# Later chunks of A in four column groups, seven combine-weight transposes ahead of the MLP loop, conversions ahead of half steps

## The chip, the cores and the metric

The kernel runs on one core of a Trainium2 chip. The metric is device time in microseconds, the median of several runs; lower is better.

## The reference, cut to what matters

Three layers follow one another, all in 32-bit floats.

```python
x = attention(q, k, v)               # 4 batches, 8 heads, 576 tokens, head size 64; masked, strided
x = x.reshape(2304, 512)             # N = 2304 tokens, D = 512
logits = x @ phi                     # 32 slots = 8 experts x 4
slot_input = softmax(logits, axis=0).T @ x
slot_out[e] = relu(slot_input[e] @ w1[e]) @ w2[e]       # 8 experts, F = 1024
c = softmax(logits, axis=1)          # combine weights, 2304 x 32
x = c @ slot_out                     # slot_out is 32 x 512
h = relu(x @ w_in)                   # d_ff = 2048
out = (h * h) @ w_out                # 2304 x 512
```

Since x is `c @ slot_out`, the kernel never forms it for the MLP. It forms A = slot_out @ w_in, which has 32 rows and 2048 columns, and takes h = relu(c @ A).

## The kernel before, in words

**Ahead of the loop.** Attention and the slot softmax come first, then the experts, two at a time, by `layer1` and `layer2` in the order of the list `order` (line 1140). The last call, `layer2(3)`, leaves slot_out in `so`, and from it four small matmuls (line 1076) and two ScalarE copies make `soT`, slot_out transposed, in which every slot stands twice (32 + 32 columns). Fillers, matmuls whose result nobody reads, stand where TensorE waits for copies: `fill(4)` (lines 1066 and 1081) and `fill(6)` (line 1127); in the profile they are line 165.

**A in chunks.** A is made in four chunks of 512 columns, numbered c. `a_chunk(c, tag)` (line 1113) multiplies `soT` (64 columns, both copies) with the chunk's w_in tiles `wi[c]` in two column groups (line 1120), and ScalarE and VectorE leave `A4[c]`: in its upper 64 rows A rounded to fp32r, twice, and in its lower 64 rows the remainder, twice (lines 1133 and 1135). Chunk 0 is made ahead of the loop in two parts, the chunk c+1 inside it, after step 8 of the twelve steps of chunk c (line 1247).

**Combine weights.** `c_parts(chf, b)` (line 1005, GpSimd, two copies) lays out the weights of batch b, rounded part and remainder side by side, in a tile `c4` of which there are two. `c_transpose(b, t0, t1)` (line 1011) transposes them on TensorE (line 1016) and one copy (line 1020) puts them into `cT4`. The list `CP` (line 1139) holds the eight calls, two for each batch. Three come ahead of the loop, the other five after the steps 0, 1, 4, 5 and 6 (`TR`, line 1173).

**The loop.** There are 48 steps n (line 1214): four chunks c, three blocks `sb` of 768 tokens, and in each block four tiles f of 128 rows of d_ff. One step is 18 matmuls of line 1229: six token tiles t, and for each the products rounded x rounded, rounded x remainder, remainder x rounded. What a step multiplies was made by `emit_h` (line 1180) in two halves of 384 tokens each: one matmul of A with cT (line 1190), then ScalarE for relu, square and rounding (lines 1197, 1203, 1205), then VectorE for the remainder (line 1206). Halves are made ahead: at t = 1 and t = 4 of step n those of step n+1 (second half) and n+2 (first half).

**Conversions.** The weights come as 64-bit floats. `conv_late` (line 1107) turns one tile into 32 bits: one GpSimd instruction into a scratch tile nm (line 220; two such tiles) and three of VectorE (lines 223, 224, 227); I call these four a conversion. For a tile of w_out `conv_split` (line 1100) later splits it on GpSimd into rounded part and remainder (lines 1104 and 1105), which the step that uses it first waits for. There is one conversion in each of eight of the twelve steps of a chunk (`CONV`, line 1174): the four tiles of w_in for the next chunk at the steps 2, 4, 5, 6, then w_out tiles at 8, 9, 10 and, for the fourth step of the next chunk, at its step 1. From step 2 on they are issued at t = 4, behind the half made there.

**Order.** From `layer2(3)` on, `pin` (line 100) makes every compute engine issue its instructions in the order in which the code names them, except those between a `pin()` and a `pin(free=True)`, which the scheduler may place: the first three transposes (line 1158) are such. So an instruction that waits holds up all behind it on its engine.

Of the kernel before, what the change touches and what calls it, by code (L numbers as in the profile page):

```python
# [7 lines left out]
F32 = mybir.dt.float32  # L8
F32R = mybir.dt.float32r
# [28 lines left out]
def kernel(  # L38
# [61 lines left out]
    def pin(free=False):  # L100
        traced = nc.cur_bb.bb.instructions
        for i in traced[mark[0]:]:
            if free or i.engine not in COMPUTE:
                continue
            prev = last_of.get(i.engine)
            if prev is not None:
                tc.add_manual_dep(
                    i, prev,
                    mybir.DependencyInfo(mybir.DependencyClass.NoSync, mybir.DependencyReason.DATA),
                    reason="issue order",  # L110
                )
            last_of[i.engine] = i.name
        mark[0] = len(traced)
# [14 lines left out]
    def psum(tag):  # L128
        n = nt[tag] = nt.get(tag, -1) + 1
        return banks[:, 2 * ("s", "o", "t1", "t2").index(tag) + n % 2]  # L130
# [31 lines left out]
    def fill(n, ins):  # L162
        ps = psum("s")
        for _ in range(n):
            new = nc.tensor.matmul(
                out=ps[:, 0:256], lhsT=identb, rhs=fillb, start=True, stop=True
            )
            behind(new, ins)
            ins = new
# [160 lines left out]
    wi = {}  # L330
# [674 lines left out]
    def c_parts(chf, b):  # L1005

        c4 = c4s[b] = tail.tile([128, 5, 2, 2, 32], F32, tag="c4", name="c4", bufs=2)
        for i, src in enumerate((chf, cl_)):
            nc.gpsimd.tensor_copy(c4[:, :, :, i], src[:, 5 * b:5 * b + 5, None, :].to_broadcast([128, 5, 2, 32]))

    def c_transpose(b, t0, t1):
        c4 = c4s[b]
        ps = psum("t2")
        n = min(t1 * 128, S) - t0 * 128
        for t in range(t0, t1):
            nc.tensor.transpose(
                out=ps[:, ts(t - t0, 128)], in_=c4[:, t].rearrange("p h a s -> p (h a s)"), identity=ident
            )
        c0 = b * S + t0 * 128
        (nc.vector.tensor_copy if b == 0 else nc.scalar.copy)(out=cT4[:, c0:c0 + n], in_=ps[:, 0:n])  # L1020


    hTs, acc2 = {}, []
# [24 lines left out]
    def layer2(pr):  # L1048
        hT = hTs.pop(pr)
        if pr == 0:  # L1050
            acc2.extend(psum("t1") for _ in range(2))
        if pr == NP - 1:
            so = tail.tile([128, 512], F32, tag="hs", name="so", bufs=2)
        for f2 in range(2):
            for i in range(2):
                for fc in (2 * f2, 2 * f2 + 1):
                    for g in range(4):
                        w = wt[("w2", 2 * pr + g // 2, 2 * (g % 2) + f2)]
                        c0 = 512 * (fc % 2) + 256 * i
                        ins = nc.tensor.matmul(  # L1060
                            out=acc2[i][ts(g, 32), 0:256], lhsT=hT[:, fc, ts(g, 32)], rhs=w[:, c0:c0 + 256],
                            start=(pr == 0 and fc == 0), stop=(pr == NP - 1 and fc == 3),
                            tile_position=(0, 32 * g),
                        )
                if (pr, f2, i) == (NP - 1, 1, 1):
                    fill(4, ins)
                if pr == NP - 1 and f2:
                    nc.scalar.copy(out=so[:, ts(i, 256)], in_=acc2[i][:, 0:256])
            done(*[("w2", 2 * pr + ee, 2 * fh + f2) for ee in range(2) for fh in range(2)])
            fetch()  # L1070
        if pr < NP - 1:
            return
        for i in range(2):
            ps = psum("o")
            for k in range(2):
                ins = nc.tensor.matmul(
                    out=ps[:, ts(k, 64)], lhsT=so[:, ts(2 * i + k, 128)],
                    rhs=same[:, 0:2].rearrange("p a s -> p (a s)"), start=True, stop=True,
                )
            if i:  # L1080
                fill(4, ins)
            nc.scalar.copy(out=soT[:, 2 * i:2 * i + 2].rearrange("p k a s -> p (k a s)"), in_=ps[:, 0:128])


    split = []
# [21 lines left out]
    def conv_late(early=False):  # L1107
        if todo or early:
            (conv_in if todo[0][0] == "in" else lambda: conv_out(early))()
            fetch()  # L1110


    def a_chunk(c, tag, n0=0, n1=2):
        two = tag == "o"
        pss = [psum(tag)[:, 0:(n1 - n0) * 128] for _ in range(1 + two)]
        both = [(n, ii) for n in range(n0, n1) for ii in (((0,), (1,)) if two else ((0, 1),))]
        for n, ii in both:
            for kt in range(KD):
                for i in ii:
                    ins = nc.tensor.matmul(  # L1120
                        out=pss[i * two][ts(i, 64), ts(n - n0, 128)],
                        lhsT=soT[:, kt].rearrange("p a s -> p (a s)"),
                        rhs=wi[c][kt][:, ts(2 * n + i, 128)],
                        start=(kt == 0), stop=(kt == KD - 1), tile_position=(0, 64 * i),
                    )
        if c == 0 and n0 == 0:
            fill(6, ins)
        if n0 == 0:
            A4[c] = mp.tile([128, 512], F32R, tag="A4", name="A4", bufs=2)
        cv = A4[c].rearrange("p (s i w) -> p i s w", i=2, w=128)[:, :, n0:n1]  # L1130
        pv = [p.rearrange("p (s w) -> p s w", w=128) for p in pss]
        for i in range(2):
            nc.scalar.copy(out=cv[0:64, i], in_=pv[i * two][ts(i, 64)])
        for i in range(2):
            nc.vector.tensor_tensor(
                out=cv[64:128, i], in0=pv[i * two][ts(i, 64)], in1=cv[0:64, i].bitcast(F32), op=ALU.subtract
            )

    CP = [(b, t0, t1) for b in range(B) for t0, t1 in ((0, 3), (3, 5))]
    for layer, pr in order:  # L1140
        if (layer, pr) == (2, NP - 1):

            pin(free=True)
            conv_late(True)
        (layer1, layer2)[layer - 1](pr)
        if (layer, pr) == (2, 0):
            chf = c_softmax()
            for b in range(2):
                c_parts(chf, b)
# [6 lines left out]
    cT4 = mp.tile([128, NT], F32R, name="cT4")  # L1156
    for x in CP[0:3]:
        c_transpose(*x)
    pin(free=True)
    part = mp.tile([128, NT // 128, 512], F32, name="part")  # L1160
    A4 = {}
    conv_split()
# [7 lines left out]
    seq = [(c, sb, QF * c + j) for c in range(NC) for sb in range(NSB) for j in range(QF)]  # L1170
    gs = {}

    TR = (0, 1, 4, 5, 6)
    CONV = [j for j in range(1, 3 * QF - 1) if j % QF != QF - 1]


# [30 lines left out]

    emit_h()
    conv_late()
    c_parts(chf, 2)  # L1210
    emit_h()
    a_chunk(0, "t1", 1, 2)
    acc = None
    for n, (c, sb, f) in enumerate(seq):
        gh, gl = gs.pop(n)
        first, last = f % QF == 0, f % QF == QF - 1
        j = n % (NSB * QF)
        if first:
            acc = [psum(a) for a in ("s", "s", "o", "o", "t1", "t1")]
        for t in range(TB):  # L1220
            if t == 1 or t == (5 if n == 0 else 4) or (n, t) == (0, 3):
                emit_h()
            if t == 1:
                conv_split()
            elif t == (2 if n < 2 else 4):
                if n < QF - 2 or j in CONV:
                    conv_late()
            for k, (a, w) in enumerate(((gh, 0), (gh, 1), (gl, 0))):
                nc.tensor.matmul(  # L1229
                    out=acc[t], lhsT=a[:, ts(t, 128)], rhs=wo[f][:, ts(w, 512)],  # L1230
                    start=(first and k == 0), stop=(last and k == 2),
                )
            if not last:
                continue

            r = sb * TB + t
            pt = part[:, r]
            nh = 2 if n == len(seq) - 1 and t == TB - 1 else 1
            for i in range(nh):
                cs = ts(i, 512 // nh)  # L1240
                if c == 0:
                    (nc.vector.tensor_copy if t % 2 else nc.scalar.copy)(out=pt, in_=acc[t])
                else:
                    nc.vector.tensor_tensor(out=pt[:, cs], in0=acc[t][:, cs], in1=pt[:, cs], op=ALU.add)  # L1244
                if c == NC - 1:
                    nc.sync.dma_start(out=out[128 * r:128 * r + 128, cs], in_=pt[:, cs])
        if j == 3 * QF - 4 and c < NC - 1:
            a_chunk(c + 1, "t2")
        if n == 3:
            c_parts(chf, 3)  # L1250
        if n in TR:
            c_transpose(*CP[3 + TR.index(n)])
    pin()


# [28 lines left out]
```

## Time and profile before

| | |
|---|---|
| median of 3 runs | 415.74 us (413.55 to 416.15) |
| the profiled execution | 418.53 us, of which 416.8 us from first to last instruction |
| busy: TensorE, VectorE, ScalarE, GpSimd | 387.3, 242.6, 226.7, 90.8 us |
| TensorE clock granted, mean | 0.979 of full speed |
| matmuls of line 1229 | 864, 218.3 us busy |
| DMA traffic | 69.88 MB |

PE is TensorE's matmuls, PEld its weight loads, DVE is VectorE, ACT ScalarE, POOL GpSimd, SP the queue that issues the DMAs. Matmuls overlap, so that their busy times can add up to more than the time that passed; the chain of waits gives the time that passed. The loop lasts from 186 to 410 us. In a stage that TensorE fills, work on another engine counts only where TensorE waits for it.

### The profile page before, as it was taken

The page shows a single profiled execution, that of the slowest core. Times are in us where ns is not written, and L with a number is a line of the kernel's source. Part 1 is how long each engine was busy: PE and PEld are TensorE (multiplying, and loading weights), DVE is VectorE, ACT ScalarE, POOL GpSimd, SP SyncE. Part 2 cuts the span into 40 slices and gives each one's busy share as a digit, 9 for nine tenths or more (in the row PEclk, how much of TensorE's full clock was granted, in tenths as well). Part 3 has the DMA queues.
Part 4 walks back from the last instruction along what each step waited for, and adds up shares of the span by engine and source line. Part 5 has one row for each costly group of instructions (what it writes and reads, how often), then busy time and mean ns, then how long its engine had stood idle before and what let it go on. Part 6 is the DMA issues. An engine that isn't in the chain of part 4 may idle for free.

```text
span 416.8 us, 9152 instructions
## 1 busy us (share of the span) xinstructions
PE 387.3 (93%) x3654; PEld 302.3 (73%) x3654; DVE 242.6 (58%) x453; ACT 226.7 (54%) x459; POOL 90.8 (22%) x128
## 2 busy tenths in 40 slices
PE   6887798889699899999999999999999999999996
PEld 3776576777587645467788887888887888878884
DVE  6565547765265561138866564867657776745434
ACT  3452627536345220039778686666666676666760
POOL 6302211112022020035600252111414103420000
PEclk9998979999799999999999999999999999999999
DMA  6898898998999999997212131221000000003033
GB/s 153 234 251 227 215 227 300 210 293 203 274 384 270 395 333 417 417 417 309 87 64 102 51 103 58 95 101 50 2 0 1 2 0 2 1 0 153 37 116 151
DMA packets 52203, 69.88 MB, mean 168 GB/s; under 512 B 31744, under 2 KB 37120, under 8 KB 52160
## 3 DMA queue, kind: packets, MB, share of 16 engines
q1 hardware_dynamic: 52160, 69.29, 52.2%
q8 instruction: 29, 0.48, 0.5%
q14 instruction: 14, 0.11, 0.1%
HBM read 64.55 MB, written 4.72 MB: 166 GB/s over the span
## 4 chain that ended last, share of the span: by engine, by line
PE 73%; DMA 9%; DVE 5%; POOL 4%; ACT 3%; SPq 3%; issue 2%; POOLq 0%; DVEq 0%; ACTq 0%
PE banks L1229 43%; DMA space<-in_v_dram 6%; PE banks L1060 4%; PE banks L1190 4%; PE banks L1030 3%; PE banks L501 2%; DMA w<-in_moe_w_dram 2%; PE banks L554 2%; PE banks L1120 2%; PE banks L665 1%; PE banks L673 1%; POOL w L1105 1%; PE banks L728 1%; PE banks L734 1%; POOL space L410 1%
## 5 line engine op out<-in xcount | busy, mean ns | idle before, releaser
L1229 PE MATMUL banks<-w 128*128 128x512 f32 x864 | 218.3, 394 | 1.6 <-POOL w L1105 1.2
L1229 PEld LDWEIGHTS banks<-w 128*128 128x128 f32 x864 | 159.3, 188 | 37.2 <-POOL w L1105 2.9
L1206 DVE TENSOR_TENSOR w<-r,w 128x384 fp32r<-128x384 f32 (+1 forms) x97 | 57.8, 598 | 72.4 <-ACT w L1205 72.3
L1197 ACT ACTIVATE r<-banks 128x384 f32<-128x384 f32 (+1 forms) x96 | 47.0, 490 | 53.0 <-PE banks L1190 43.6
L1203 ACT ACTIVATE r<-r 128x384 f32<-128x384 f32 (+1 forms) x96 | 50.3, 524 | 3.0
L1205 ACT CAST w<-r 128x384 fp32r<-128x384 f32 (+1 forms) x97 | 49.5, 510 | 4.1 <-DVE r L1202 0.5
L488 ACT COPY space<-banks 64x576 f32<-64x576 f32 (+2 forms) x64 | 34.8, 543 | 19.5 <-PE banks L153 12.2
L220 POOL TENSOR_SCALAR nm<-w 128x512 f32<-128x512 f32 x28 | 23.5, 843 | 63.0 <-DMA w<-in_moe_w_out_dram 31.9
L1244 DVE TENSOR_TENSOR part<-banks,part 128x512 f32<-128x512 f32 (+1 forms) x55 | 34.9, 673 | 2.4 <-PE banks L1229 2.3
L410 POOL COPY space<-space 32x1088 f32<-32x1088 f32 x16 | 17.5, 1096 | 80.9 <-DMA space<-in_v_dram 57.6
L1104 POOL CAST w<-wf 128x512 fp32r<-128x512 f32 x16 | 11.8, 740 | 94.8 <-PE banks L1229 37.2
L1190 PE MATMUL banks<-cT,A 128*128 128x384 f32 x96 | 32.0, 335 | 0.0
L501 PE MATMUL banks<-ident,space 128*128 128x128 f32 x128 | 21.9, 297 | 1.6 <-DMA space<-in_q_dram 1.6
L224 DVE SCALAR_TENSOR_TENSOR nm<-w,nm 128x512 uint32<-128x512 uint32 x32 | 22.3, 696 | 1.1
L223 DVE TENSOR_SCALAR nm<-nm 128x512 uint32<-128x512 uint32 x32 | 14.6, 457 | 12.5 <-POOL nm L220 8.7
L1105 POOL TENSOR_TENSOR w<-wf,w 128x512 fp32r<-128x512 f32 x16 | 21.4, 1339 | 1.4
L525 ACT ACTIVATE space<-banks 128x576 f32<-128x576 f32 x16 | 10.4, 651 | 20.1 <-PE banks L506 15.9
L1190 PEld LDWEIGHTS banks<-cT,A 128*128 128x128 f32 x96 | 18.0, 188 | 3.9 <-ACT r L1197 0.2
L488 DVE COPY space<-banks 128x576 f32<-128x576 f32 (+1 forms) x16 | 9.7, 608 | 17.3 <-ACT space L488 13.5
L501 PEld LDWEIGHTS banks<-ident,space 128*128 128x128 f32 x128 | 15.7, 159 | 4.7 <-POOL w L437 2.5
L665 PE MATMUL banks<-space 128*32 128x130 f32 x288 | 13.0, 294 | 5.6 <-POOL space L410 3.7
L665 PEld LDWEIGHTS banks<-space 128*32 128x32 f32 x288 | 9.5, 116 | 7.7 <-POOL space L410 4.7
(186 smaller groups left out, 450.4 us busy)
## 6 DMA issues: line engine op xcount, KB each, us to landing
w<-in_moe_w_dram SPq DMA_DIRECT2D x48, 512.0 KB, 7.3
w<-in_moe_w_in_dram SPq DMA_DIRECT2D x16, 512.0 KB
space<-in_moe_w_dram SPq DMA_DIRECT2D x16, 512.0 KB, 7.4
w<-in_moe_w_out_dram SPq DMA_DIRECT2D x16, 512.0 KB, 6.6
space<-in_v_dram SPq DMA_DIRECT2D x32, 144.0 KB, 7.5
out_dram<-part SPq DMA_DIRECT2D x17, 256.0 KB, 2.0
space<-in_k_dram SPq DMA_DIRECT2D x16, 128.0 KB, 2.9
space<-in_q_dram SPq DMA_DIRECT2D x16, 128.0 KB, 2.6
```

Source lines behind the costliest of these rows:

```text
L220: nc.gpsimd.tensor_scalar(out=m, in0=hf, scalar1=2.0 ** -112, scalar2=1.0, op0=ALU.mult, op1=ALU.mult)
L488: return (nc.scalar.copy if act else nc.vector.tensor_copy)(out=out, in_=in_)
L501: nc.tensor.transpose(out=pf[:, w * t:w * t + 128], in_=m[:, ts(t, 128)], identity=ident)
L665: nc.tensor.matmul(out=pv[c, n // 4] if n < 18 else pv[c, 4].rearrange("p (h e) -> p h e", h=2), lhsT=w, rhs=i, start=True, stop=True, til ...
L1105: nc.gpsimd.tensor_tensor(out=lo, in0=r, in1=hi.bitcast(F32), op=ALU.subtract)
L1190: nc.tensor.matmul(out=ps[:, 0:HB], lhsT=A4[c][:, ts(f % QF, 128)], rhs=cT4[:, c0:c0 + HB], start=True, stop=True)
L1197: nc.scalar.activation(out=r[:, cuts[0]], in_=ps[:, cuts[0]], func=AF.Relu)
L1203: nc.scalar.activation(out=r[:, cuts[0]], in_=r[:, cuts[0]], func=AF.Square)
L1205: nc.scalar.copy(out=gh[:, x], in_=r[:, x])
L1206: nc.vector.tensor_tensor(out=gl[:, x], in0=r[:, x], in1=gh[:, x].bitcast(F32), op=ALU.subtract)
L1229: nc.tensor.matmul(out=acc[t], lhsT=a[:, ts(t, 128)], rhs=wo[f][:, ts(w, 512)], start=(first and k == 0), stop=(last and k == 2),)
L1244: nc.vector.tensor_tensor(out=pt[:, cs], in0=acc[t][:, cs], in1=pt[:, cs], op=ALU.add)
```

## The change

It makes chunks 1 to 3 of A in another way, moves three of the transposes (and the `c_parts` that two of them need) ahead of the loop, where they take the place of fillers, and turns the order of two calls inside a step.

- `a_next(c)` takes the place of `a_chunk` in the loop: 16 matmuls of 32 weight columns in four column groups, one ScalarE copy (hi), one VectorE subtraction (lo), and 16 GpSimd copies of 32 x 128 that lay hi, hi, lo, lo of each group into the four row blocks of `A4[c]`. It is issued at t = 3 of step 7 of the twelve.
- `slots_out(so)` holds what stood at the end of `layer2`; the call `CP[3]` takes the place of the first `fill(4)`, `CP[4]` comes where the second stood, and `CP[5]` with `fill(2)` takes the place of `fill(6)`. Their copies out of the bank are issued a little later on ScalarE. `c_parts(chf, 2)` moves ahead of them. In the loop only `CP[6]` and `CP[7]` remain, after steps 5 and 6.
- At t = 4 (and t = 1) the order is now split, conversion, half, where it was half, then split or conversion.

```diff
+    def slots_out(so):
+        later = []
+        c_transpose(*CP[3], "s", later)
         for i in range(2):
             ps = psum("o")
             for k in range(2):
-                ins = nc.tensor.matmul(
+                nc.tensor.matmul(
                     out=ps[:, ts(k, 64)], lhsT=so[:, ts(2 * i + k, 128)],
                     rhs=same[:, 0:2].rearrange("p a s -> p (a s)"), start=True, stop=True,
                 )
-            if i:
-                fill(4, ins)
             nc.scalar.copy(out=soT[:, 2 * i:2 * i + 2].rearrange("p k a s -> p (k a s)"), in_=ps[:, 0:128])
+        c_transpose(*CP[4], "s", later)
+        for x in later:
+            x()
...
+        later = []
         if c == 0 and n0 == 0:
-            fill(6, ins)
+            c_transpose(*CP[5], "s", later)
+            fill(2, ins)
...
+    def a_next(c):
+        ps = psum("t2")[:, 0:128]
+        for kt in range(KD):
+            for g in range(4):
+                nc.tensor.matmul(
+                    out=ps[ts(g, 32)], lhsT=soT[:, kt, 0, :], rhs=wi[c][kt][:, ts(g, 128)],
+                    start=(kt == 0), stop=(kt == KD - 1), tile_position=(0, 32 * g),
+                )
+        A4[c] = mp.tile([128, 512], F32R, tag="A4", name="A4", bufs=2)
+        hi = mp.tile([128, 128], F32R, tag="Ah", name="Ah", bufs=1)
+        lo = mp.tile([128, 128], F32R, tag="Al", name="Al", bufs=1)
+        nc.scalar.copy(out=hi, in_=ps)
+        nc.vector.tensor_tensor(out=lo, in0=ps, in1=hi.bitcast(F32), op=ALU.subtract)
+        for g in range(4):
+            for n, x in enumerate((hi, hi, lo, lo)):
+                nc.gpsimd.tensor_copy(A4[c][ts(n, 32), ts(g, 128)], x[ts(g, 32)])
...
     for x in CP[0:3]:
         c_transpose(*x)
+    c_parts(chf, 2)
     pin(free=True)
+    slots_out(so)
...
-    TR = (0, 1, 4, 5, 6)
+    TR = (5, 6)
...
     conv_late()
-    c_parts(chf, 2)
     emit_h()
...
         for t in range(TB):
+            if (j, t) == (2 * QF - 1, 3) and c < NC - 1:
+                a_next(c + 1)
+            if t == 1:
+                conv_split()
+            if t == (2 if n < 2 else 4) and (n < QF - 2 or j in CONV):
+                conv_late()
             if t == 1 or t == (5 if n == 0 else 4) or (n, t) == (0, 3):
                 emit_h()
-            if t == 1:
-                conv_split()
-            elif t == (2 if n < 2 else 4):
-                if n < QF - 2 or j in CONV:
-                    conv_late()
...
-        if j == 3 * QF - 4 and c < NC - 1:
-            a_chunk(c + 1, "t2")
         if n == 3:
             c_parts(chf, 3)
         if n in TR:
-            c_transpose(*CP[3 + TR.index(n)])
+            c_transpose(*CP[6 + TR.index(n)])
```

## Rows read from the trace of the kernel before

**Rows 1.** Page: busy us of each engine, share of the span, instructions.
```profile
PE 387.3 (93%) x3654; PEld 302.3 (73%) x3654; DVE 242.6 (58%) x453; ACT 226.7 (54%) x459; POOL 90.8 (22%) x128
```

**Rows 2.** By stage: us, busy of PE, PEld, DVE, ACT, POOL (instructions), clock, DMA.
```profile
176.00:185.00 9.00, 9.00 (x108) 5.94 (x106) 3.10 (x7) 2.28 (x7) 2.32 (x3) 1.00 1.03 419
185.00:203.00 18.00, 17.31 (x90) 13.03 (x88) 14.46 (x24) 14.26 (x32) 10.63 (x13) 1.00 0.68 268
203.00:253.00 50.00, 50.00 (x251) 41.34 (x250) 31.54 (x54) 38.08 (x77) 13.66 (x16) 1.00 0.22 74
```

**Rows 3.** Chain of waits in the loop: start us, us, what.
```profile
221.20 0.22 PE banks L1016 x2
...
230.37 1.90 PE banks L1120 x32
...
242.13 0.17 PE banks L1190
242.30 2.07 PE banks L1229 x9
```

**Rows 4.** Timeline of PE, halves around `a_chunk` and a fourth step: start us, us.
```profile
228.64 0.33 PE L1190 MATMUL banks<-cT,A 128*128 128x384 f32 x1
...
232.99 0.34 PE L1190 MATMUL banks<-cT,A 128*128 128x384 f32 x1
...
257.65 0.33 PE L1190 MATMUL banks<-cT,A 128*128 128x384 f32 x1
260.50 0.33 PE L1190 MATMUL banks<-cT,A 128*128 128x384 f32 x1
```

**Rows 5.** Chain of waits ahead of a fourth step.
```profile
255.69 0.43 DVE nm L223
...
257.69 0.81 POOL w L1104
...
258.59 1.29 POOL w L1105
...
259.92 0.73 PE banks L1229 x2
```

**Rows 6.** Timeline, all engines, ahead of that step: start us, us, engine, instruction.
```profile
246.47 1.03 DVE L1206 TENSOR_TENSOR w<-r,w 128x384 fp32r<-128x384 f32 x1
...
247.05 0.96 POOL L220 TENSOR_SCALAR nm<-w 128x512 f32<-128x512 f32 x1
...
252.93 0.56 DVE L1206 TENSOR_TENSOR w<-r,w 128x384 fp32r<-128x384 f32 x1 [1.68 <-ACT w L1205]
```

**Rows 7.** Chain of waits in attention: 32-column weights, 128 columns streamed, four groups.
```profile
119.55 1.01 PE banks L734 x32
```

**Rows 8.** Chain of waits from the last expert into the loop.
```profile
181.15 0.54 PE banks L165 x4
...
184.48 0.76 PE banks L165 x6
...
186.22 0.69 DVE r L1202
```

**Rows 9.** Chain of waits ahead of step 3.
```profile
201.13 1.49 POOL w L1105
```

**Rows 10.** POOL's groups by shape: instruction xcount, busy us, mean ns of one.
```profile
L410 POOL COPY space<-space 32x1088 f32<-32x1088 f32 x16 | 17.5, 1096 | 80.9 <-DMA space<-in_v_dram 57.6 <-PE banks L503 12.7 <-PE banks L506 10.2
...
L437 POOL TENSOR_SCALAR_AFFINE_SELECT w<-w 32x36 f32<-32x36 f32 x4 | 1.6, 398 | 0.2
...
L480 POOL COPY phi<-phi 128x384 f32<-128x384 f32 x1 | 0.5, 506 | 1.8 <-DMA phi<-in_moe_phi_dram 1.8
L476 POOL MEMSET space<- 128x64 f32 x4 | 0.4, 157 | 0.0
```

**Rows 11.** Timeline of DVE: last instruction of the last w_in conversion, start us, us.
```profile
223.13 0.69 DVE L227 SCALAR_TENSOR_TENSOR w<-w,nm 128x512 uint32<-128x512 uint32 x1
```

**Rows 12.** Timeline of POOL: first instruction of the third w_out conversion.
```profile
241.90 0.96 POOL L220 TENSOR_SCALAR nm<-w 128x512 f32<-128x512 f32 x1
```

More of the change, by code (lines that the diff above doesn't have):

```diff
@@ L1009, in c_parts, with c_transpose @@
             nc.gpsimd.tensor_copy(c4[:, :, :, i], src[:, 5 * b:5 * b + 5, None, :].to_broadcast([128, 5, 2, 32]))
-    def c_transpose(b, t0, t1):
+    def c_transpose(b, t0, t1, tag="t2", later=None):
         c4 = c4s[b]
-        ps = psum("t2")
+        ps = psum(tag)
         n = min(t1 * 128, S) - t0 * 128
@@ L1019, in c_transpose, with out_of_bank @@
         c0 = b * S + t0 * 128
-        (nc.vector.tensor_copy if b == 0 else nc.scalar.copy)(out=cT4[:, c0:c0 + n], in_=ps[:, 0:n])
+        def out_of_bank():
+            (nc.vector.tensor_copy if b == 0 else nc.scalar.copy)(out=cT4[:, c0:c0 + n], in_=ps[:, 0:n])
+        if later is None:
+            out_of_bank()
+        else:
+            later.append(out_of_bank)
     hTs, acc2 = {}, []
@@ L1064, in layer2 @@
                         )
-                if (pr, f2, i) == (NP - 1, 1, 1):
-                    fill(4, ins)
                 if pr == NP - 1 and f2:
@@ L1070, in layer2 @@
             fetch()
-        if pr < NP - 1:
-            return
+        if pr == NP - 1:
+            return so
+    def slots_out(so):
+        later = []
+        c_transpose(*CP[3], "s", later)
         for i in range(2):
@@ L1079, in layer2 @@
                 )
-            if i:
-                fill(4, ins)
             nc.scalar.copy(out=soT[:, 2 * i:2 * i + 2].rearrange("p k a s -> p (k a s)"), in_=ps[:, 0:128])
+        c_transpose(*CP[4], "s", later)
+        for x in later:
+            x()
     split = []
@@ L1137, in a_chunk @@
             )
+        for x in later:
+            x()
+    def a_next(c):
[14 more added lines that the diff above has]
+                nc.gpsimd.tensor_copy(A4[c][ts(n, 32), ts(g, 128)], x[ts(g, 32)])
     CP = [(b, t0, t1) for b in range(B) for t0, t1 in ((0, 3), (3, 5))]
@@ L1144 @@
             conv_late(True)
-        (layer1, layer2)[layer - 1](pr)
+        so = (layer1, layer2)[layer - 1](pr)
         if (layer, pr) == (2, 0):
```

## The prediction

> **What bounds the kernel now.** Read the engines' shares first [rows 1]: TensorE is busy 93% of the span, no other engine above 58%. The stages [rows 2] say where that holds: from 203 us on the sum for PE equals the time that passes, at the full clock; from 185 to 203 us 0.7 us of PE time is open, and there VectorE (14.5 of 18) and GpSimd (10.6) matter; up to 185 us the DMA engines are full (share 1.03), so nothing the change moves can come before the last expert's weights. The chain of waits [rows 3] gives the loop's beat: a half is nine matmuls, 2.07 us, and one of line 1190, 0.17 us: 2.24 us, and a step 4.48 us. 96 halves make 215 us, which the change leaves alone. What is open in the loop are the places where the distance of two halves is not 2.24 us. The timeline of PE [rows 4] shows two kinds. Around `a_chunk` the distance is 4.35 us, three times in the loop, of which the chain gives 1.90 us to its 32 records [rows 3]. At the fourth step of chunks 1, 2 and 3 it is 2.85 us (the three lie within 0.05 us): 0.6 us of waiting. The chain ahead of such a step [rows 5] says for what: the split of a w_out tile (lines 1104, 1105) ends at 259.88 us and the step's second product starts at 259.92.
>
> **The later chunks of A.** Three times 32 records in two groups go, 1.90 us each [rows 3]. Their successor has as many records, 16 matmuls of two records each, but half the weight columns, so that four run beside one another. The trace has that very shape in attention: 32 records, 32-column weights, 128 columns streamed, 1.01 us [rows 7]. I take it; the ends are 0.95 us (half of 1.90) and 1.90 us (no more overlap than now). Gain 3 x 0.89 = 2.67 us. It now comes 1.5 steps earlier and needs the chunk's last w_in tile, whose conversion ends at 223.82 us [rows 11] in step 7 of chunk 0, about when `a_next` is issued. The change itself moves that conversion ahead of a half (below), some 2 us, so I cost the wait at nothing; without that cover it would be up to 0.5 us a chunk.
>
> **Conversions ahead of halves.** Ahead of the waiting step GpSimd's part was done at 248.01 us, but VectorE's three instructions start at 255.69 us [rows 5, 6], because in program order they stand behind the remainder (line 1206) of the half issued at the same t, which ScalarE delivers at 255.2. Put ahead of it, they can follow the remainder before, which ends at 253.49 us [rows 6]: 2.2 us earlier. The split then ends near 257.7 us instead of 259.88, and the step needs it at 259.3. All three waits go: 3 x 0.58 = 1.75 us. What is late next: the remainder that now stands behind the conversion. The half made at t = 4 is used 1.33 steps, 6.0 us, later; its own chain (matmul to remainder) takes 2.5 us, so it can lose 3.5 us, and a conversion whose GpSimd part is done costs it 1.9 us. The danger is a conversion whose GpSimd part is not done: VectorE then waits with every remainder queued behind it.
>
> **The sixteen GpSimd copies.** They are new, and they stand on GpSimd's queue ahead of the first w_out conversion of the next chunk. The trace has no 32 x 128 copy. Two copies give a line: 1.096 us for 1088 columns, 0.506 for 384 [rows 10], so 0.84 ns a column and 0.18 us fixed: 0.29 us for 128. The ends are 0.10 us (four memsets of 64 columns in 0.4 us) and 0.40 us (the small selects on 32 partitions) [rows 10]; I take 0.29, as the rows nearest in kind are copies. From the start of step 7: the matmuls run at 2.24 to 3.25 us, ScalarE's copy and VectorE's subtraction (about 0.3 us each, an estimate from the 0.56 us of a 384-column remainder [rows 6], and VectorE has other work between) bring lo at about 4.8; fourteen copies are then left, 4.1 us, done at 8.9. Step 8 starts at 5.5. So GpSimd is free 3.4 us into step 8, or about 4.0 with two collisions with remainders: during a GpSimd instruction a remainder took 1.03 us instead of 0.56, and the GpSimd instruction behind it stretched too [rows 6]. Then comes the series conversion, split, conversion, split, conversion; one round lasts 5.15 us (247.05 less 241.90 [rows 6, 12]), longer than a step. The third conversion begins 3.4 to 4.0 plus 10.3 us into step 8, that is 3.6 to 4.2 us ahead of the new chunk's first step at 17.9; now it begins 4.0 us ahead (241.90, with that step at 245.9 by the beat). GpSimd is thus as late as before, but the remainder that the new step needs first now stands behind that conversion: 0.95 + 1.9 + 0.56 = 3.4 us from its start. It arrives 0.2 to 0.8 us before its step, with the last tiles' sums of the old chunk behind it. I cost 0.2 us a chunk, 0.6 in all; the ends are 0 and what 0.40 us a copy would cost, 16 x 0.11 = 1.8 us a chunk, 5.3 in all. A rule bears on this. The Trainium skill (SBUF — State Buffer, two separate sides) says that GpSimd and a VectorE instruction with two SBUF inputs exclude each other for the whole instruction. The stretched rows agree; by the rule each of some three remainders in those 5 us could hold a copy up for its full 0.56 us, 1.7 us a chunk, and the sum would be 5.2 less 5.1 us, no gain.
>
> **The transposes.** `CP[5]` leaves step 4: two transposes, 0.22 us [rows 3]. `CP[3]` and `CP[4]` leave steps 0 and 1, which gains nothing by itself: step 3 waits anyway for GpSimd's split of the fourth w_out tile, up to 202.6 us [rows 9], and that series is set by the conversions. It begins earlier only if the first half does. There the fillers of 0.54 and 0.76 us [rows 8] become two transposes (0.22) and two transposes with two fillers (about 0.45), the middle one three transposes instead of 0.44 us. The small matmuls behind the first filler need only the first part of `so`, ready by then; behind the last, the copies of A end soon after, so I count 0.45 us of the 0.7. The copies out of the banks fall into ScalarE's waits. `c_parts(2)` leaves GpSimd at 186 us, where VectorE's multiplication beside it took 0.69 us for 256 columns [rows 8]; a like one takes 0.56 for 384 [rows 6]: up to 0.25 us more. It goes to about 176 us, where GpSimd has nothing to do. Together 0.6 us, ends 0 and 0.9.
>
> **Sum.** 2.67 + 1.75 + 0.22 + 0.6 - 0.6 = 4.6 us. The profiled execution, 418.53 us, would become 413.9; the median of the runs lies 2.8 us below it, so 415.74 becomes 411.1.
>
> **Rivals.** *Copies too slow.* This is the one on the other side. Each 0.1 us more for a copy delays GpSimd 1.6 us a chunk, and from there VectorE and the new chunk's first halves, 4.8 us in all. The gain without this item is 5.2 us, so it is gone at 0.39 us a copy; at 0.48 the kernel is 3.9 us slower, about 419.6. For it speak the selects at 0.40 and the collisions; against it the two copies on one line. Short of the tipping point, at 0.33 to 0.38, it gives 412.5 to 415.5. *The waits at the fourth steps stay*, because VectorE loses the 2.2 us elsewhere (with GpSimd later, its series is): 412.9. *The four groups do not overlap:* 1.90 us stays, 413.8; the rows of attention speak against it. *Copies issued closely,* 0.2 us, and the whole of the start: 410 or a little less.
>
> **How the numbers follow.** Chances: forecast (410 to 412.4) 0.50; slow copies short of tipping 0.20; slow copies beyond it 0.08; waits stay 0.07; groups 0.05; better than forecast 0.10. The likeliest time is 411.1. The range goes from 409.4 (the better case, with a start at its upper end) to 415.2, which leaves the tipped case and the ends out. A change below 1%, 4.2 us, cannot be told from none here. 411.6 lies within the forecast's own width, about six tenths of it below: 0.30 + 0.10, and some of the smaller cases with the runs' own scatter, 0.48 faster. Slower by over 1% needs 0.48 us a copy: 0.06. The rest, 0.46, lies between.
>
> **What would show it.** In the profile after: `a_next` on the chain with 1.0 us; no distance of two halves near 2.85 us at fourth steps; VectorE's line 223 there starting right behind the remainder of the half before; the sixteen copies near 0.29 us and ending before step 9; step 3's wait ending 0.6 us nearer to the last expert than now. I am wrong if the copies take over 0.35 us, or if TensorE waits at the first steps of new chunks, with VectorE waiting for line 220 before them.

## The result, and the profile after

Over 20 runs of each, the changed kernel takes 411.56 us (median, 407.76 to 417.25) and the kernel before 416.38 us (411.35 to 420.75). The ratio is 0.9904, interval 0.9877 to 0.9931: 4.0 us less, between 2.9 and 5.1. The ratio is taken from the faster of two states of executions alone, so it need not equal the ratio of the medians; the profiles of the kernel before and of e8 are of slower executions, whose surplus lies ahead of the stretches read below (there the granted clock is 1.00 and the beat 2.24 us, as in the others). The forecast was 411.1 us, a gain of 4.6.

The profiled executions differ by more, 416.8 and 408.4 us of span, and most of what goes beyond 4.0 us has nothing to do with the change. In the chains of waits the last expert's matmuls end at 181.15 us before and at 177.49 us after: 3.66 us of the 8.4 come from attention and its transfers, which both kernels do alike (in a second profile of the changed kernel, e11, that end lies at 173.99 us). I therefore read two stretches of each trace: from that end to the end of the span (235.65 us before, 230.91 after), and from the first half made in step 3 to the end (213.58 and 209.56). The first difference is 4.74 us, the second 4.02.

The page's line of the engines, and the same stages by busy time (columns as in [rows 2]; the windows begin 4 us earlier, as the first half does, and the last one is 46 us long, not 50):

```profile
PE 381.5 (93%) x3639; PEld 297.8 (73%) x3642; DVE 241.1 (59%) x450; ACT 225.3 (55%) x456; POOL 107.1 (26%) x176
```

```profile
172.00:181.00 9.00, 9.00 (x110) 6.49 (x107) 3.05 (x7) 2.93 (x10) 2.87 (x5) 1.00 1.03 419
181.00:199.00 18.00, 16.89 (x85) 12.80 (x84) 13.86 (x24) 13.82 (x31) 10.55 (x12) 1.00 0.73 288
199.00:245.00 46.00, 46.00 (x235) 37.61 (x234) 30.47 (x51) 35.47 (x72) 18.64 (x31) 1.00 0.22 77
```

GpSimd (POOL) has 16 us more to do than before [rows 1], TensorE 6 us less. The loop is still TensorE's, at the same beat; 181 to 199 us still has a hole, of 1.1 us.

The chain of waits in the loop, to be read against [rows 3] and [rows 7]; line 1157 is `a_next`, 1223 the half's matmul (1190 before), 1262 the step's (1229 before):

```profile
219.30 1.01 PE banks L1157 x32
...
241.37 0.17 PE banks L1223
241.54 2.07 PE banks L1262 x9
```

The four groups take 1.01 us, what the like shape took in attention, not 1.90.

The timeline of PE around `a_next` and at a fourth step, against [rows 4]:

```profile
217.56 0.34 PE L1223 MATMUL banks<-cT,A 128*128 128x384 f32 x1
221.03 0.34 PE L1223 MATMUL banks<-cT,A 128*128 128x384 f32 x1
...
252.41 0.33 PE L1223 MATMUL banks<-cT,A 128*128 128x384 f32 x1
254.65 0.33 PE L1223 MATMUL banks<-cT,A 128*128 128x384 f32 x1
```

3.47 us between the halves where it was 4.35, 2.24 us where it was 2.85; both three times.

VectorE and GpSimd ahead of that fourth step (timeline), against [rows 5, 6]:

```profile
247.68 0.56 DVE L1239 TENSOR_TENSOR w<-r,w 128x384 fp32r<-128x384 f32 x1 [1.68 <-ACT w L1238]
248.16 0.42 DVE L223 TENSOR_SCALAR nm<-nm 128x512 uint32<-128x512 uint32 x1
...
250.16 0.82 POOL L1114 CAST w<-wf 128x512 fp32r<-128x512 f32 x1 [7.49 <-PE banks L1262]
251.06 1.30 POOL L1115 TENSOR_TENSOR w<-wf,w 128x512 fp32r<-128x512 f32 x1
```

Line 223 follows the remainder of the half before at once, and the split ends at 252.4 us, 1.5 us ahead of the step (by the beat it begins at 253.95).

The timeline of GpSimd after `a_next`; a row of line 1168 is a pair of copies:

```profile
220.70 0.61 POOL L1168 CAST A<-Ah 32x128 fp32r<-32x128 f32 x2 [11.87 <-ACT Ah L1164]
...
225.56 0.86 POOL L1168 CAST A<-Al 32x128 fp32r<-32x128 f32 x2
226.50 0.66 POOL L220 TENSOR_SCALAR nm<-w 128x512 f32<-128x512 f32 x1
...
231.55 0.65 POOL L220 TENSOR_SCALAR nm<-w 128x512 f32<-128x512 f32 x1
...
236.59 0.64 POOL L220 TENSOR_SCALAR nm<-w 128x512 f32<-128x512 f32 x1
```

The copies last 5.7 us; GpSimd is free 3.8 us into step 8 (which begins at 222.6), and the series of conversions follows in rounds of 5.04 us.

Two places where the change costs something. The first is the entry of chunk 2, the first halves of the new chunk, beside which VectorE adds the old chunk's sums from the banks to `part` (line 1277), the evacuation that frees each bank. Timelines of PE and VectorE; the step begins at 295.7:

```profile
293.97 0.33 PE L1223 MATMUL banks<-cT,A 128*128 128x384 f32 x1
296.37 0.33 PE L1223 MATMUL banks<-cT,A 128*128 128x384 f32 x1
...
292.49 0.43 DVE L223 TENSOR_SCALAR nm<-nm 128x512 uint32<-128x512 uint32 x1 [1.80 <-POOL nm L220]
...
294.29 0.55 DVE L1239 TENSOR_TENSOR w<-r,w 128x384 fp32r<-128x384 f32 x1
294.75 0.68 DVE L1277 TENSOR_TENSOR part<-banks,part 128x512 f32<-128x512 f32 x1
```

VectorE waits 1.8 us for GpSimd's line 220, with a remainder and the first evacuation of a bank behind it; the halves then are 2.40, 2.36 and 2.29 us apart: 0.33 us lost, at chunk 3 as well, at chunk 1 nothing. The second is step 4 of chunk 0:

```profile
203.34 0.33 PE L1223 MATMUL banks<-cT,A 128*128 128x384 f32 x1
205.77 0.33 PE L1223 MATMUL banks<-cT,A 128*128 128x384 f32 x1
...
198.86 0.65 DVE L223 TENSOR_SCALAR nm<-nm 128x512 uint32<-128x512 uint32 x1 [1.78 <-POOL nm L220]
...
202.85 1.29 DVE L1275 COPY part<-banks 128x512 f32<-128x512 f32 x2
```

There the conversion of the first w_in tile stands ahead of a half and waits for GpSimd, which still splits the fourth w_out tile; the evacuations come late and cost 0.19 us.

The start, in the chain of waits, against [rows 8, 9]:

```profile
181.13 0.19 PE banks L1223
...
182.11 0.44 DVE r L1235
...
196.75 1.48 POOL w L1115
```

The first half is 3.64 us behind the last expert, 4.09 before; the multiplication beside which `c_parts` ran takes 0.44 us, not 0.69; step 3's second product starts 20.78 us behind the expert, 21.51 before.

### The profile page after: what moved, and what is told of

Read it like the earlier page. It is cut to its first block, busy times and chain, and to the rows that moved or that the text cites. A ratio compares the mean times of both kernels' runs of the same rounds, so it can differ in the third digit from the quotient of the medians.

```text
span 408.4 us, 9170 instructions
## 1 busy us (share of the span) xinstructions
PE 381.5 (93%) x3639; PEld 297.8 (73%) x3642; DVE 241.1 (59%) x450; ACT 225.3 (55%) x456; POOL 107.1 (26%) x176
## 4 chain that ended last, share of the span: by engine, by line
PE 79%; DVE 7%; DMA 4%; ACT 4%; POOL 3%; issue 2%; SPq 1%; DVEq 0%; POOLq 0%; ACTq 0%
PE banks L1262 46%; PE banks L1223 4%; DMA space<-in_v_dram 4%; PE banks L1067 4%; PE banks L1037 3%; PE banks L501 3%; PE banks L554 2%; PE banks L665 2%; PE banks L795 1%; PE banks L728 1%; PE banks L734 1%; PE banks L673 1%; PE banks L506 1%; ACT space L488 1%; PE banks L574 1%
## 5 line engine op out<-in xcount | busy, mean ns | idle before, releaser
L1239 DVE TENSOR_TENSOR w<-r,w 128x384 fp32r<-128x384 f32 (+1 forms) x97 | 58.8, 613 | 55.2 <-ACT w L1238 54.9
L220 POOL TENSOR_SCALAR nm<-w 128x512 f32<-128x512 f32 x28 | 21.9, 784 | 26.9 <-DVE w L227 14.7
L1114 POOL CAST w<-wf 128x512 fp32r<-128x512 f32 x16 | 12.9, 807 | 50.7 <-PE banks L1262 29.3
L1115 POOL TENSOR_TENSOR w<-wf,w 128x512 fp32r<-128x512 f32 x16 | 23.1, 1443 | 1.4
L1168 POOL CAST A<-Ah 32x128 fp32r<-32x128 f32 x24 | 7.5, 313 | 35.4 <-ACT Ah L1164 34.3
```

Of the source, the lines that this page charges most:

```text
L220: nc.gpsimd.tensor_scalar(out=m, in0=hf, scalar1=2.0 ** -112, scalar2=1.0, op0=ALU.mult, op1=ALU.mult)
L1115: nc.gpsimd.tensor_tensor(out=lo, in0=r, in1=hi.bitcast(F32), op=ALU.subtract)
L1239: nc.vector.tensor_tensor(out=gl[:, x], in0=r[:, x], in1=gh[:, x].bitcast(F32), op=ALU.subtract)
```

## The experiments

All stretches are from each kernel's own profile, one for each; "from expert" and "from step 3" are the two defined above. The ratio is time to that of the kernel before, with its interval; e4 has two executions, the others 11 or more.

| kernel | from expert, us | from step 3, us | ratio |
|---|---|---|---|
| before | 235.65 | 213.58 | |
| changed | 230.91 | 209.56 | 0.9904 (0.9877 to 0.9931) |
| e1 groups alone | 235.17 | 213.13 | 0.9994 (0.9938 to 1.0049) |
| e2 order alone | 233.88 | 211.85 | 0.9934 (0.9882 to 0.9986) |
| e3 transposes alone | 234.71 | 213.36 | 0.9991 (0.9950 to 1.0033) |
| e4 copies twice | 247.55 | 226.21 | 1.0306 (1.0241 to 1.0370) |
| e5 two groups there | 233.00 | 211.65 | 0.9971 (0.9932 to 1.0010) |
| e6 hi on ScalarE | 231.29 | 209.94 | 0.9919 (0.9888 to 0.9950) |
| e7 second early | 232.00 | 209.59 | 0.9981 (0.9947 to 1.0014) |
| e8 hi spread | 230.20 | 208.86 | 0.9888 (0.9844 to 0.9932) |
| e9 second in parts | 230.53 | 209.57 | 0.9910 (0.9864 to 0.9957) |
| e10 spread and parts | 230.02 | 208.91 | 0.9924 (0.9873 to 0.9975) |
| e11 changed again | 231.81 | 209.53 | 0.9884 (0.9840 to 0.9929) |

**One part alone: e1, e2, e3.** To the kernel before, e1 adds only `a_next` (the function is as in the change; shown is its call), e2 only the order of calls, e3 only the moved transposes.

```diff
# e1
+            if (j, t) == (2 * QF - 1, 3) and c < NC - 1:
+                a_next(c + 1)
...
-        if j == 3 * QF - 4 and c < NC - 1:
-            a_chunk(c + 1, "t2")
```

> The kernel before with the four column groups and their sixteen GpSimd copies alone (issued in step 7), transposes and order of calls as before. Measured from the end of the last expert's matmuls to the end of the span, which took 235.65 us before and 230.9 us after. Theory 1 (the parts hold one another up): TensorE gains 3 x 0.88 = 2.65 us, but the matmuls now wait 0.3 to 0.6 us a chunk for the last w_in tile, whose conversion still stands behind a half, the waits at fourth steps stay, and the first steps of chunks lose some 0.3 to 0.5 us each: 234.0 to 235.3. Theory 2 (the parts add up on TensorE's time): 233.0.

235.17 us, a gain of 0.48: the second theory falls. That the first one's range holds is in part luck, for two of its terms were off in opposite directions. The matmuls waited for no w_in tile (the halves around them are 3.44 to 3.47 us apart, as in the changed kernel): the tile that is converted last is multiplied in the last quarter only. The entries of chunks 2 and 3 lost more than the 0.3 to 0.5 us expected, 1.1 and 1.2 us. The timelines of VectorE and PE at the entry of chunk 2:

```profile
292.87 1.68 DVE L1223 TENSOR_TENSOR w<-r,w 128x384 fp32r<-128x384 f32 x1 [0.59 <-ACT w L1222]
295.10 0.43 DVE L223 TENSOR_SCALAR nm<-nm 128x512 uint32<-128x512 uint32 x1 [0.54 <-POOL nm L220]
...
296.89 0.68 DVE L1263 TENSOR_TENSOR part<-banks,part 128x512 f32<-128x512 f32 x1
...
295.36 0.33 PE L1207 MATMUL banks<-cT,A 128*128 128x384 f32 x1
...
298.50 0.34 PE L1207 MATMUL banks<-cT,A 128*128 128x384 f32 x1
```

Here the remainder goes ahead of the conversion, is held up by GpSimd's split (1.68 us instead of 0.56), and the evacuation of the first bank ends at 297.57 us, after the new step should have begun; the halves are 3.14 us apart.

```diff
# e2
+            if t == 1:
+                conv_split()
+            if t == (2 if n < 2 else 4) and (n < QF - 2 or j in CONV):
+                conv_late()
             if t == 1 or t == (5 if n == 0 else 4) or (n, t) == (0, 3):
                 emit_h()
-            if t == 1:
-                conv_split()
-            elif t == (2 if n < 2 else 4):
-                if n < QF - 2 or j in CONV:
-                    conv_late()
```

> The kernel before with the order of calls alone (split, conversion, half). Theory 1: the three waits at fourth steps go, 1.75 us, and nothing comes in their place, since GpSimd's part of those conversions is done in time: 233.7 to 233.9 us from the last expert to the end, no distance of two halves near 2.8 us. Rival: the conversions only trade places with the remainders, which are then late themselves: 235.2 to 235.7.

233.88 us, as the first theory has it: the three waits at fourth steps are gone, and step 4 pays the 0.18 us seen above (2.42 us between its halves). The rival falls. The timeline of PE at the fourth step of chunk 1 and at the entry of chunk 2:

```profile
252.65 0.33 PE L1190 MATMUL banks<-cT,A 128*128 128x384 f32 x1
254.89 0.33 PE L1190 MATMUL banks<-cT,A 128*128 128x384 f32 x1
...
297.34 0.33 PE L1190 MATMUL banks<-cT,A 128*128 128x384 f32 x1
299.58 0.33 PE L1190 MATMUL banks<-cT,A 128*128 128x384 f32 x1
```

The second pair shows what the theory did not name: the entries of chunks 2 and 3, which lost 0.27 us together in the kernel before, lose nothing here. So the 1.77 us are 1.75 at the fourth steps, with step 4's loss about made up by the entries.

e3 is the changed kernel with the loop as before:

```diff
# e3, against the changed kernel
-            if (j, t) == (2 * QF - 1, 3) and c < NC - 1:
-                a_next(c + 1)
+            if t == 1 or t == (5 if n == 0 else 4) or (n, t) == (0, 3):
+                emit_h()
             if t == 1:
                 conv_split()
-            if t == (2 if n < 2 else 4) and (n < QF - 2 or j in CONV):
-                conv_late()
-            if t == 1 or t == (5 if n == 0 else 4) or (n, t) == (0, 3):
-                emit_h()
+            elif t == (2 if n < 2 else 4):
+                if n < QF - 2 or j in CONV:
+                    conv_late()
...
+        if j == 3 * QF - 4 and c < NC - 1:
+            a_chunk(c + 1, "t2")
```

> The kernel before with the transposes moved ahead of the loop alone. Theory 1: the wait of step 3 ends 0.5 to 0.8 us nearer to the last expert (21.5 us before) and step 4 loses 0.22 us: 234.6 to 234.9 us to the end. Rival: that wait is set by the arrival of the weights and not by what was moved, and only the 0.22 us come: 235.4.

234.71 us, a gain of 0.94: 0.72 us up to step 3, 0.22 us behind it. The three parts alone give 0.48 + 1.77 + 0.94 = 3.2 us, together 4.74. Of the missing 1.55 us about 1.4 are the entries of chunks 2 and 3: they lose 0.27 us before, 2.3 in e1, nothing in e2, and 0.66 in the changed kernel. The copies thus cost 2.0 us there in the old order and 0.66 in the new one. The groups pay only because the order of calls is changed with them.

**The GpSimd copies: e4, e6, e8.** e4 makes each copy twice.

```diff
# e4
-                nc.gpsimd.tensor_copy(A4[c][ts(n, 32), ts(g, 128)], x[ts(g, 32)])
+                for _ in range(2):
+                    nc.gpsimd.tensor_copy(A4[c][ts(n, 32), ts(g, 128)], x[ts(g, 32)])
```

> The changed kernel with each of the sixteen GpSimd copies of a later chunk made twice, which leaves the result alone. They were spaced 0.33 us, so GpSimd is free 5.3 us later in each of three chunks. Theory 1 (no slack left: GpSimd's series of conversions, with the remainders behind it on VectorE, sets when a new chunk can start): 4.5 to 5.3 us lost a chunk, 244.5 to 247 us from the last expert to the end against 230.9, with TensorE waiting already in steps 10 and 11, for remainders behind a line 223 that waits for line 220. Rival (the copies are hidden work, the 0.33 us at the entries come from VectorE's evacuations alone): below 233.

247.55 us, 16.6 more, a little beyond the range. The timelines of GpSimd, VectorE and PE in chunk 0:

```profile
231.22 1.33 POOL L1169 CAST A<-Al 32x128 fp32r<-32x128 f32 x4
232.64 0.64 POOL L220 TENSOR_SCALAR nm<-w 128x512 f32<-128x512 f32 x1
...
233.31 0.43 DVE L223 TENSOR_SCALAR nm<-nm 128x512 uint32<-128x512 uint32 x1 [7.07 <-POOL nm L220]
...
235.71 0.50 PE L1263 MATMUL banks<-w 128*128 128x512 f32 x1 [3.18 <-DVE w L1240]
```

VectorE stands 7.07 us in front of line 223, remainders behind it, and TensorE waits 3.18 us for one. The copies last 11.5 us instead of 5.7, 5.8 more a chunk, and 5.5 us of it reach the end: there is next to no slack left behind them. The mechanism of *Copies too slow*, the rival on the other side in the prediction, is real; its price is not reached at 0.31 us a copy.

e6 moves the eight hi copies to ScalarE in one block, e8 the same eight, two behind each of the next four halves.

```diff
# e6
-                nc.gpsimd.tensor_copy(A4[c][ts(n, 32), ts(g, 128)], x[ts(g, 32)])
+                (nc.scalar.copy if n < 2 else nc.gpsimd.tensor_copy)(A4[c][ts(n, 32), ts(g, 128)], x[ts(g, 32)])
# e8: hi copies are put on a list owed; behind emit_h()
+                for _ in range(min(2, len(owed))):
+                    nc.scalar.copy(*owed.pop(0))
```

> The changed kernel with the eight copies of the rounded part (hi) on ScalarE, the eight of the remainder left on GpSimd. Theory 1: GpSimd is free some 2.6 us earlier a chunk and the waits at the entries of chunks 2 and 3, 0.33 us each, go: 230.2 to 230.5 us from the last expert to the end. Rival: eight ScalarE copies of some 0.2 us in the step in which ScalarE also empties banks make the halves late: 231 to 232.5.

231.29 us, the rival's figure. The entries behave as the first theory says (2.24 us each), but a new wait of 0.53 us stands at steps 20 to 21 and 32 to 33. ScalarE and PE:

```profile
275.49 2.46 ACT L1168 CAST A<-Ah 32x128 fp32r<-32x128 f32 x8
...
280.34 0.33 PE L1223 MATMUL banks<-cT,A 128*128 128x384 f32 x1
280.91 2.36 PE L1262 MATMUL banks<-w 128*128 128x512 f32 x9 [0.24 <-DVE part L1277]
283.11 0.33 PE L1223 MATMUL banks<-cT,A 128*128 128x384 f32 x1
```

The block holds up the next half on ScalarE, its remainder on VectorE, and the evacuation queued behind that. A copy takes 0.31 us on ScalarE, not the 0.2 of the expectation.

> The changed kernel with the eight hi copies on ScalarE as before, but two of them behind each of the four halves that follow, where ScalarE has 0.6 us free, not eight in one block of 2.46 us. Theory 1 (the block made the half late that waited 0.53 us at step 21, and the entries are GpSimd's doing): no distance of two halves above 2.3 us at the entries nor one step after the copies; 230.2 to 230.5 us from the last expert to the end. Rival: ScalarE has no room in any form, and a wait of 0.3 to 0.5 us a chunk stays: 230.9 to 231.5.

230.20 us, and no distance above 2.26 us at the entries or behind the copies: from step 3 on 0.70 us less than the changed kernel, the 2 x 0.33 us of the entries. In four pairs of about 0.60 us a chunk the copies fit ScalarE's gaps, for instance

```profile
282.39 0.60 ACT L1267 CAST A<-Ah 32x128 fp32r<-32x128 f32 x2
```

**Place or groups: e5.** In the changed kernel `a_chunk(c + 1, "t2")` stands where `a_next(c + 1)` is called, so two groups and no GpSimd copies.

> The changed kernel, but with the former two groups for the later chunks of A, at the new place in step 7 and without GpSimd copies. Theory 1: TensorE pays 3 x 0.88 us again, the waits at the first steps of chunks 2 and 3 (0.33 us each now) go: 232.8 to 233.2 us from the last expert to the end, against 230.9. Rival: the copies cost as much as the groups save, and the place alone brought the gain: 230.5 to 231.3.

233.00 us: 1.90 us of matmuls in the chain again, the entries without a wait, as the first theory has it.

```profile
220.97 1.90 PE banks L1130 x32
```

**The hole in steps 0 to 3: e7, e9.** e7 calls `conv_late()` for the second w_out tile ahead of `conv_split()` and chunk 0 of A; e9 puts its four instructions into gaps one by one.

```diff
# e7
+    conv_late()
     conv_split()
     a_chunk(0, "o", 0, 1)
...
     emit_h()
-    conv_late()
     emit_h()
# e9, steps = the four instructions of that conversion
+    steps[0]()
     conv_split()
+    steps[1]()
     a_chunk(0, "o", 0, 1)
+    steps[2]()
...
     emit_h()
-    conv_late()
+    steps[3]()
     emit_h()
```

> The changed kernel with the conversion of the second w_out tile issued ahead of the first split and of chunk 0 of A, not behind the first half. Theory 1 (what is left open at 181 to 199 us is GpSimd's and VectorE's series of the first four w_out tiles): the series runs 3 us earlier, the wait at step 3 (0.85 us) and that in step 1 (0.66 us) go, against some 0.6 to 0.9 us by which VectorE's subtractions for A come later: 229.9 to 230.6 us from the last expert to the end. Rival: the start is on the path and nothing comes back: 231.4 to 231.8.

232.00 us, worse than the rival's range. Both halves of the theory are seen: from step 1 to step 3 the halves keep the beat (the wait in step 3 is 0.17 us), but the start costs 2.3 us (the end of the first half, against the expert's end) and not 0.9, because VectorE's conversion ran beside GpSimd's split (timeline of VectorE):

```profile
184.03 1.64 DVE L227 SCALAR_TENSOR_TENSOR wf<-w,nm 128x512 uint32<-128x512 uint32 x1
185.69 0.61 DVE L1147 TENSOR_TENSOR A<-banks,A 64x128 fp32r<-64x128 f32 x2
```

Line 227 takes 1.64 us instead of 0.69, beside a split (line 1115) of 1.58 us on GpSimd, and A's subtraction waits behind it.

> The changed kernel with the conversion of the second w_out tile taken apart: its GpSimd instruction ahead of the first split, VectorE's first instruction ahead of chunk 0 of A, the second behind A's subtractions, the third behind the first half, in gaps that VectorE has. Theory 1 (steps 0 to 3 wait for the series of conversions): the series runs about 1 us earlier, the wait at step 3 (0.85 us) goes and that in step 1 (0.66 us) shrinks, against 0.2 to 0.4 us at the start: 230.0 to 230.6 us from the last expert to the end. Rival: every VectorE instruction ahead of the first half delays it in full, as when the whole conversion was put there: 231.2 to 232.

230.53 us, within the first theory's range, near its upper end. The wait in step 1 is gone (2.26 us), the one at step 3 stays at 0.8 us, since TensorE reaches it earlier; and again an instruction beside the split is stretched, line 230 of that kernel (224 in the changed one) from 0.69 to 1.28 us.

> Both of these together. Theory 1: they touch different stages and add up: 229.4 to 230.1 us from the last expert to the end, some 0.3 per cent below the changed kernel. Rival: one eats the other: 230.4 or more.

230.02 us: the two gains, 0.71 and 0.38, nearly add up, to 0.89. Of it 0.65 us are gained from step 3 on and 0.24 ahead of it, where e9 gained 0.39; here the second w_out tile, whose conversion was moved, landed 1.95 us behind the expert's end, in e9 0.75 us.

> The changed kernel itself, beside the three others on the same chip. Both theories: 0.988 to 0.993 of the kernel before, and 230.7 to 231.2 us from the last expert to the end in its profile, if that measure does not depend on what attention took.

0.9884, as expected, and from step 3 on 209.53 us, 0.03 from the first profile. The stretch from the expert was missed, 231.81: it does depend on the transfers. The timelines of GpSimd and VectorE:

```profile
174.91 0.66 POOL L220 TENSOR_SCALAR nm<-w 128x512 f32<-128x512 f32 x1 [4.61 <-DMA w<-in_moe_w_out_dram]
...
176.86 0.69 DVE L227 SCALAR_TENSOR_TENSOR wf<-w,nm 128x512 uint32<-128x512 uint32 x1
177.58 0.61 DVE L1147 TENSOR_TENSOR A<-banks,A 64x128 fp32r<-64x128 f32 x2
```

Here the first w_out tile landed 0.9 us behind the expert's end (173.99), in the first profile 0.65 us ahead of it, and A's subtraction stood behind its conversion. In all the other profiles of the table it came 0.63 to 0.74 us ahead, so they can be compared; but the 0.72 us up to step 3, and the gain of e9, hold for that landing alone. How often it is late in the timed executions is not known.

By time, e6, e8, e9, e10 and the changed kernel cannot be told apart; their intervals overlap. None is shown to beat the changed kernel.

## Why the prediction was right, step by step

- **The later chunks of A**, 2.67 us: measured 4.35 + 4.36 + 4.35 less 3.47 + 3.46 + 3.47, 2.66 us. The row of attention was the right row. The clause that the w_in tile would cost up to 0.5 us a chunk without the turned order was wrong (e1: 3.44 to 3.47 us between the halves, no wait).
- **Conversions ahead of halves**, 1.75 us: 2.85 + 2.80 + 2.82 less 3 x 2.24, 1.75 us, and the waits are gone in e2 too. The bill left out two terms: step 4, 0.19 us, where the conversion placed first waits for GpSimd (the prediction named just that danger, but put no price on it), and the 0.27 us that the turned order saves at the entries (e2). That the two nearly cancel is luck.
- **The sixteen copies**: 0.29 us forecast, 0.31 measured (0.33 from start to start). GpSimd was to be free 3.4 to 4.0 us into step 8: 3.8 us in chunk 0, 4.1 in chunk 1. Cost 0.6 us forecast; the entries lose 0.66 us, and nothing where the order is the same but GpSimd has no copies (e5) or half of them (e8). So TensorE did wait at the first steps of two new chunks, with VectorE waiting for line 220 ahead of them, which the prediction had named as a sign of being wrong; the wait has the size that its sum had priced. e4 shows the slope: 16 more copies, 5.5 us a chunk for 5.8 us of copies; by it 0.1 us more on each copy would cost 1.5 us a chunk, near the 1.6 of the rival, but no run has single copies near its tipping point of 0.39 us.
- **Lock or no lock.** The rule of the Trainium skill (SBUF — State Buffer, two separate sides), that GpSimd and a VectorE instruction with two SBUF inputs exclude each other, is borne out by the stretched instructions of e1 (1.68 us instead of 0.56), e7 (1.64 instead of 0.69) and e9 (1.28 instead of 0.69), each beside a split of 1.27 to 1.58 us on GpSimd. Its cost here was mis-sized by the upper bound: in each chunk two pairs of copies took 0.83 to 0.86 us instead of 0.61, about 0.5 us in all and not 1.7. The 0.6 us of two collisions in the prediction was near.
- **The transposes**: 0.22 us in step 4, and 0.6 us at the start; measured 0.22 (e3) and 0.72, made of 0.45 us for the first half and 0.25 us for the multiplication beside `c_parts`. Both sizes are as worked out, but the 0.45 came another way: in the chain two transposes took 0.37 us, not 0.22, and two with two fillers 0.59, not 0.45.
- **Sum**: from step 3 on 2.67 + 1.75 + 0.22 - 0.6 = 4.04 us forecast, 4.02 in the profile; term by term the halves give 2.66 + 1.75 + 0.22 - 0.19 + 0.27 - 0.66 = 4.05. To it comes the start, 0.6 forecast and 0.72 in the profile: 4.6 and 4.74. The executions gave 4.0 us (2.9 to 5.1), which does not tell 4.0 from 4.7.

## What to carry to other kernels

When an instruction is moved ahead on an in-order engine, price the wait it may bring along, and what stands behind it there: here turning two calls gained 1.77 us by itself (e2) and saved some 1.4 us more of what the GpSimd copies cost (e1 against the changed kernel). Work given to an engine that looks idle (GpSimd, 22% busy before) is not hidden if a series of instructions on it sets the next stage's start (e4); look up when that series must begin and not how busy the engine is. Read a small gain from a stretch of the trace that starts behind the transfers: the spans of two profiles of the same kernel lie 2.6 us apart here (408.4 and 405.8), the stretch from step 3 0.03 us.

## What the runs showed of the hardware that was not expected

- Line 220 on GpSimd took 0.63 to 0.66 us in the rounds of the changed kernel, in which VectorE stood in front of line 223, and 0.96 us in the same rounds before, in which VectorE worked beside it. In the same rounds the split's second instruction (line 1115) took mostly 1.47 to 1.48 us instead of 1.29, so that the round fell only from 5.15 to 5.04 us.
- ScalarE's copies of 32 x 128 from SBUF take as long as GpSimd's: eight in 2.46 us, 0.31 each (e6).
